# Expert halves by seven products in a third expert, sums kept in PSUM, and float64 weights narrowed through DRAM

## The chip, the cores and the metric

The kernel runs on one core of one Trainium2 chip. The metric is device time in microseconds (us) of one execution, as the median of several runs. Engines are named as in the profile: PE is TensorE (matmul), PEld its weight load, DVE is VectorE, ACT is ScalarE, POOL is GpSimd, SP is the engine whose queue issues all DMAs here.

## The reference, cut to what matters

Blocked causal attention over 4 x 8 heads of 576 rows, then a mixture of four experts in which every token goes through every expert, then a second layer with a softmax-gated activation and a layer norm.

```
x = attention(q, k, v)                        # 2304 tokens x 512
p = domain_probs / sum(domain_probs)
for e in range(4):
    out += p[:, e] * (relu(x @ w1[e]) @ w2[e])    # w1[e]: 512 x 1024, w2[e]: 1024 x 512
h = out @ w_in                                # w_in: 512 x 1024, float64
solu = h * softmax(h)
ln = (solu - mean) / sqrt(var + 1e-6) * g_ln
result = ln @ w_out                           # w_out: 1024 x 512, float64
```

## The kernel before, in words

Tokens are 18 tiles of 128. Every product is done in three float16 products (high x high, high x low, low x high), since each float32 operand x is kept as hi = f16(x) and lo = f16(x - hi). Attention makes the token tiles one after the other; the experts work on tiles that are ready. The tiles are two parts (`PARTS`): 6 tiles in two groups of 3, then 12 tiles in four groups of 3. A phase j is one expert on one part: phases 0 to 3 are experts 0 to 3 on the first part, phases 4 to 7 are experts 0 to 3 on the second part (`e = j % E`). Phases 0 to 3, and part of 4, run beside the attention; from about 450 us on only the experts are left, and from 928 us the second layer (`m2_h`, `m2_o`).

In a plain phase (`phase_units`, 0 to 4 and 7) a group of 384 tokens needs 8 x 12 matmuls of 384 columns for the first product (`emit_h`, L311) and three times 24 matmuls of 512 columns for the second (`emit_o`, L331). ACT takes the relu out of PSUM (L319), DVE the low part (L320), and DVE adds each finished output tile into `acc` (L355).

Phases 5 and 6 (experts 1 and 2) do the first product by halves (`st_units`, L529): both operands are cut in two along rows and columns, and seven products of half the size in each direction stand in for eight, so a group needs 2 chains x 7 products x 12 matmuls of 192 columns. The combined operands are made ahead: `T` from the tokens, once per group (`t_steps`), and `S` from the expert's split weights, once per expert and chain (`s_steps`). Each product has a PSUM tile of its own; DVE adds them up in SBUF (tiles `stu`, seven adds per chain, L541), ACT takes the relu of each result (L547) and DVE its low part (L548), 128 columns x 192 at a time.

Weights are loaded into one staging tile in four parts, squared and scaled on first use, and split by ACT (hi, L263) and DVE (lo, L266) into one of three slots (`w0` to `w2`) that rotate by the counter in `next_w`. All eight phases load both matrices of their expert. `w_in` and `w_out` come as 64-bit words; during phase 7 DVE turns them into float32 in eight pieces of 128x1024 with seven instructions each (L189 to L213).

DMAs are all issued by SP in order, and an issue waits until what it depends on is done, so a waiting issue holds up those behind it. The instruction order of each engine is written out when the program is built: a list scheduler takes instructions by priority and by when their inputs should be ready, and `spread` sets between which units of a phase a background task stands. Relu, low parts and sums have a raised priority (`high_priority`).

Of the kernel before, what the change touches and what calls it, by code (L numbers as in the profile page):

```python
# [7 lines left out]
F32 = mybir.dt.float32  # L8
# [34 lines left out]
GT = 3  # L43

# [14 lines left out]
def tile_kernel(  # L59
# [46 lines left out]
    hp = ctx.enter_context(tc.tile_pool(name="h", bufs=8))  # L106
# [52 lines left out]
    cv = {}  # L159

    def w_steps(key, src, bits, inv, tag, load_eng, rows=None, hi_eng=None, place_raw="stage", known=False):

        n = src.shape[1]
        k = src.shape[0] // 128
        q = k // 4

        wide = src.dtype == I64
        raw = {}

        def load64(c):  # L170
            def f():
                r = cv["pool"].tile([128, 1024, 2], I32, tag="raw64", name="raw64")
                dv = src.bitcast(I32).rearrange("(k p) f -> p k f", p=128)
                load_eng.dma_start(
                    out=r.rearrange("p (k f) w -> p k (f w)", k=q), in_=dv[:, c * q:(c + 1) * q]
                )
                raw[c] = r
            return f

        def to32(c):  # L180

            a = [None, None]

            def words():
                r = raw[c]
                a[0] = cv["pool"].tile([128, 1024], I32, tag="cvA", name="cvA")
                a[1] = cv["pool"].tile([128, 1024], I32, tag="cvP", name="cvP")
                h = r[:, :, 1]
                vec.tensor_scalar(  # L189
                    out=a[0], in0=h, scalar1=3, scalar2=0x3FFFFFF8,  # L190
                    op0=ALU.logical_shift_left, op1=ALU.bitwise_and,
                )
                vec.scalar_tensor_tensor(
                    out=a[0], in0=h, scalar=-0x40000000, in1=a[0], op0=ALU.bitwise_and, op1=ALU.bitwise_or
                )
                vec.tensor_scalar(
                    out=a[1], in0=h, scalar1=0x7FFFFFFF, scalar2=None, op0=ALU.bitwise_and
                )

            def value():  # L200
                top, tmp = a[0].bitcast(F32), a[1].bitcast(F32)
                vec.scalar_tensor_tensor(
                    out=top, in0=a[1], scalar=float(896 << 20), in1=top, op0=ALU.is_ge, op1=ALU.mult
                )
                vec.tensor_scalar(
                    out=a[1], in0=a[0], scalar1=-0x800000, scalar2=None, op0=ALU.bitwise_and
                )
                o = stage[key][:, c * 1024:(c + 1) * 1024]
                vec.scalar_tensor_tensor(
                    out=o, in0=raw.pop(c)[:, :, 0].bitcast(U32), scalar=2.0 ** -52, in1=tmp,  # L210
                    op0=ALU.mult, op1=ALU.mult,
                )
                vec.tensor_tensor(out=o, in0=o, in1=top, op=ALU.add)  # L213

            return [words, value]
# [9 lines left out]
        def load_part(c):  # L225
            def f():
                sv = stage[key].rearrange("p (k f) -> p k f", k=k)
                dv = src.rearrange("(k p) f -> p k f", p=128)
                load_eng.dma_start(out=sv[:, c * q:(c + 1) * q], in_=dv[:, c * q:(c + 1) * q])
            return f  # L230
# [22 lines left out]
        def split(c):  # L253
            def f():
                r = stage[key][:, c * 1024:(c + 1) * 1024]
                hi = wt[key][:, 0].rearrange("p k f -> p (k f)")[:, c * 1024:(c + 1) * 1024]
                lo = wt[key][:, 1].rearrange("p k f -> p (k f)")[:, c * 1024:(c + 1) * 1024]
# [18 lines left out]
        if wide:  # L276
            steps = [load64(0), load64(1), load]
            for c in range(4):
                steps += to32(c)
                if c < 2:  # L280
                    steps.append(load64(c + 2))
# [6 lines left out]

    xT, x2T, acc = {}, {}, {}
    hch = {}  # L290

# [7 lines left out]
    def emit_h(e, t0, k, fs, pool):  # L299
# [5 lines left out]
        h = hp.tile([128, 2, 128 * GT], F16, tag="h", name="hch")  # L305
# [34 lines left out]
    def out_unit(e, t, o0, pool):  # L340
        c = coef_of(e, t)
        ps = emit_o(e, o0, pool)
        k = t - PARTS[part(t)][0]
        with tc.high_priority(offset=PRI):
            if e == 0:
# [10 lines left out]
        if e == E - 1:  # L356
            finish_x2(t)

# [9 lines left out]
    def coef_of(e, t):  # L368
# [4 lines left out]
        if e == 0:  # L373
            c = sp.tile([128, 1], F32, tag="c0", name="c0")
            vec.tensor_scalar(
                out=c, in0=pt[:, t, 0:1], scalar1=c1, scalar2=c2, op0=ALU.mult, op1=ALU.mult
# [25 lines left out]
    def phase_units(j, runs, pool):  # L402

        e = j % E
        units = []
        for t0, k in runs:
# [5 lines left out]
            for t in range(t0, t0 + k):  # L412
                units.append((
                    t, lambda t=t, o=(t - t0) * 128: out_unit(e, t, o, pool), 24 * 0.216,
# [12 lines left out]
    def combine(shape, out, x, y, op):  # L427
# [7 lines left out]
        def high():  # L435
            r["f"] = view(st_["tmp"].tile([128, 512], F32, tag="f", name="stf", bufs=3))
            vec.tensor_tensor(out=r["f"], in0=x(0), in1=y(0), op=op)  # L437

        def low():
# [3 lines left out]
            if "l" not in r:  # L443
                r["l"] = view(st_["tmp"].tile([128, 512], F32, tag="l", name="stl", bufs=1))
# [8 lines left out]
    def t_steps(g):  # L453
# [8 lines left out]

        def place():
            Ts[g] = st_["keep"].tile([128, 4, 2, 2, HT], F16, tag=f"T{g}", name="T")

        sh = (2, HT)
        r1, a1 = combine(sh, T(0), B(0, 1), B(0, 0), ALU.subtract)
        r2, a2 = combine(sh, T(1), B(1, 1), lambda b: None if b else r1["f"], ALU.subtract)
        r3, a3 = combine(sh, T(2), B(1, 1), B(0, 1), ALU.subtract)
        r4, a4 = combine(sh, T(3), B(1, 0), lambda b: None if b else r2["f"], ALU.subtract)  # L470
        return [place] + a1 + a2 + a4 + a3

    def s_steps(e, half):

        def A(i, j):
            return lambda b: wt["w1", e][:, b, 2 * j:2 * j + 2, 512 * i + 256 * half:512 * i + 256 * half + 256]

        def S(k):
            return lambda b: Ss[e, half][:, k, b]
# [4 lines left out]
        sh = (2, 256)  # L484
        r1, a1 = combine(sh, S(0), A(1, 0), A(1, 1), ALU.add)
        neg = lambda b: None if b else r1["f"]
        r2 = {}

        def second():
            r2["f"] = st_["tmp"].tile([128, 512], F32, tag="f", name="stf", bufs=3).rearrange("p (a b) -> p a b", a=2)  # L490
            vec.tensor_tensor(out=r2["f"], in0=r1["f"], in1=A(0, 0)(0), op=ALU.subtract)

        def second_low():
            vec.tensor_tensor(out=r2["f"], in0=r2["f"], in1=A(0, 0)(1), op=ALU.subtract)

        def second_split():
            two_parts(r2["f"], S(1)(0), S(1)(1))

        r3, a3 = combine(sh, S(2), A(0, 0), A(1, 0), ALU.subtract)
        r4, a4 = combine(sh, S(3), A(0, 1), lambda b: None if b else r2["f"], ALU.subtract)  # L500
        return [place] + a1 + [second, second_low, second_split] + a4 + a3

    def st_units(e, g, half, pool):

        key = (1, g)
        t = GROUPS[1][g][0] + GT - 1
        fa = [2 * half, 2 * half + 1]
        fb = [4 + f for f in fa]
        ps, u = {}, {}
# [13 lines left out]
        def product(c, lhs, rhs):  # L523
            ps[c] = pool.tile([128, 512], F32, tag="h", name="hps")
# [10 lines left out]
        W = 2 * HT  # L535

        def add(k, x, y):
            n = {"s": 3, "u": 2}.get(k[0], 1)
            u[k] = st_["tmp"].tile([128, W], F32, tag=k[0] + str(n), name="stu", bufs=n)
            with tc.high_priority(offset=PRI):  # L540
                vec.tensor_tensor(out=u[k], in0=x, in1=y, op=ALU.add)  # L541

        def hidden(x, fs, j):
            with tc.high_priority(offset=PRI):
                for jj, f in enumerate(fs):
                    h, v = hch[f][:, :, HT * j:HT * j + HT], x[:, jj * HT:jj * HT + HT]
                    act.activation(out=h[:, 0], in_=v, func=AF.Relu)  # L547
                    vec.scalar_tensor_tensor(  # L548
                        out=h[:, 1], in0=v, scalar=0.0, in1=h[:, 0], op0=ALU.max, op1=ALU.subtract
                    )  # L550

        def f1():
            for f in fa + fb:
                hch.pop(f, None)
# [877 lines left out]
```

## Time and profile before

| | |
|---|---|
| median of 3 runs | 1122.9 us (1121.86 to 1125.56) |
| profiled execution | span 1118.5 us from its first to its last instruction; the page gives no time of its own for what lies around the span |
| PE busy | 1054.0 us, 94% of the span |
| DVE / ACT / POOL busy | 821.9 / 500.8 / 184.7 us |
| bytes moved by DMA | 125.87 MB, mean 113 GB/s |
| attention with phases 0 to 3 | 0 to about 447 us |
| phases 4, 5, 6, 7 | about 447 to 567, 567 to 684.5, 684.5 to 802.5, 802.5 to 928 us |
| second layer | 928 to 1118.5 us |

PE is busy almost throughout after 250 us; the first quarter of the span has gaps. A matmul's recorded duration overlaps that of the next, so counts and starts tell more about PE's speed than mean durations do. The stage borders are read from the chain of waits, in which L529 (halves) takes over from L311 (plain) and back.

### The profile page before, as it was taken

How to read it: one execution, taken by the hardware profiler on the slowest of the kernel's cores; microseconds unless marked ns; L12 is line 12 of the kernel's file. 1: busy time of each engine (PE TensorE's matmuls, PEld its weight loads, DVE VectorE, ACT ScalarE, POOL GpSimd, SP SyncE). 2: the span in 40 equal slices, each digit the busy share in tenths (PEclk: the TensorE clock that was granted, in tenths of full speed). 3: DMA queues.
4: the chain of work that ended last, by engine and by line, in shares of the span. 5: the costliest groups of instructions: out<-in, count | busy, mean ns of one | idle time of the engine just before them, and what ended most of it. 6: DMA issues, size and time to landing. Idle time of an engine off the chain costs nothing.

```text
span 1118.5 us, 19987 instructions
## 1 busy us (share of the span) xinstructions
PE 1054.0 (94%) x7776; PEld 642.1 (57%) x7776; DVE 821.9 (73%) x1818; ACT 500.8 (45%) x1115; POOL 184.7 (17%) x176
## 2 busy tenths in 40 slices
PE   4479889899998999999999999999999999999998
PEld 4456766466565555655567777766555554444443
DVE  6888787648678678536997459544999656999883
ACT  5657676647655457433542224211324332333222
POOL 4874632323115411000000000000000000000000
PEclk9999999899999999999999999999999999999999
DMA  9868986837648748332150002200422101443343
GB/s 306 236 149 176 248 183 148 246 94 209 174 103 236 152 114 224 74 43 56 33 203 6 1 1 79 73 1 1 148 87 96 38 19 29 89 90 85 76 85 85
DMA packets 216063, 125.87 MB, mean 113 GB/s; under 512 B 183712, under 2 KB 185760, under 8 KB 215456
## 3 DMA queue, kind: packets, MB, share of 16 engines
q1 hardware_dynamic: 215968, 124.59, 43.4%
q8 instruction: 61, 1.00, 0.4%
q14 instruction: 34, 0.28, 0.1%
HBM read 73.18 MB, written 6.29 MB: 71 GB/s over the span
## 4 chain that ended last, share of the span: by engine, by line
PE 73%; DVE 11%; DMA 8%; POOL 4%; issue 3%; ACT 1%; SPq 0%; DVEq 0%; ACTq 0%; POOLq 0%
PE ops L331 27%; PE hps L311 15%; PE hps L529 9%; PE h L1283 8%; PE o L1346 8%; DMA pT<-hl 6%; PE pv L872 3%; DVE wt L266 2%; DVE hl L843 1%; PE sps L799 1%; PE sps L800 1%; DVE stf L437 1%; DMA vraw<-in_vC_dram 1%; POOL wt L259 1%; DVE hch L320 1%
## 5 line engine op out<-in xcount | busy, mean ns | idle before, releaser
L331 PE MATMUL ops<-wt,hch 128*128 128x512 f16 x1728 | 387.6, 379 | 3.9 <-DVE wt L266 1.6
L331 PEld LDWEIGHTS <-hch 128*128 128x128 f16 x1728 | 166.2, 98 | 190.4 <-issue 4.4
L311 PE MATMUL hps<-xT,wt 128*128 128x384 f16 (+1 forms) x1920 | 268.5, 297 | 1.7 <-DVE hch L320 1.3
L311 PEld LDWEIGHTS <-wt 128*128 128x128 f16 x1920 | 164.0, 100 | 85.9 <-issue 4.0
L838 ACT ACTIVATE p<-sps,nm 128x320 f32<-128x320 f32 (+4 forms) x144 | 79.1, 553 | 89.9 <-DVE nm L809 59.6
L843 DVE TENSOR_TENSOR hl<-p,hl 128x320 f16<-128x320 f32 (+4 forms) x132 | 90.5, 699 | 33.2 <-ACT hl L842 32.9
L266 DVE SCALAR_TENSOR_TENSOR wt<-stage,ws,wt 128x1024 f16<-128x1024 f32 x72 | 99.7, 1392 | 8.3 <-ACT wt L263 6.9
L355 DVE SCALAR_TENSOR_TENSOR acc<-ops,coef,acc 128x512 f32<-128x512 f32 x54 | 40.4, 748 | 82.1 <-PE ops L331 82.1
L1283 PE MATMUL h<-wt,x2T 128*128 128x512 f16 x432 | 95.5, 379 | 0.8 <-DVE acc L355 0.8
L319 ACT ACTIVATE hch<-hps 128x384 f16<-128x384 f32 x130 | 62.3, 482 | 75.1 <-PE hps L311 74.6
L1346 PE MATMUL o<-wt,lt 128*128 128x512 f16 x432 | 95.5, 379 | 0.0
L320 DVE SCALAR_TENSOR_TENSOR hch<-hps,hch 128x384 f16<-128x384 f32 x130 | 70.5, 544 | 32.2 <-ACT hch L319 32.2
L799 PE MATMUL sps<-ks,qhi 128*128 128x288 f32 (+3 forms) x160 | 67.4, 424 | 23.7 <-ACT p L838 10.1
L263 ACT ACTIVATE wt<-stage,ws 128x1024 f16<-128x1024 f32 x64 | 71.1, 1140 | 6.0 <-PE hps L311 2.2
L1283 PEld LDWEIGHTS <-x2T 128*128 128x128 f16 x432 | 42.2, 98 | 52.0 <-issue 1.1
L541 DVE TENSOR_TENSOR stu<-stu,hps 128x384 f32<-128x384 f32 x112 | 59.4, 550 | 17.3 <-PE hps L529 17.3
L1346 PEld LDWEIGHTS <-lt 128*128 128x128 f16 x432 | 42.3, 98 | 50.9
L547 ACT ACTIVATE hch<-stu 128x192 f16<-128x192 f32 x128 | 39.2, 354 | 70.4 <-DVE stu L541 70.2
L842 ACT ACTIVATE hl<-p 128x320 f16<-128x320 f32 (+4 forms) x132 | 66.0, 522 | 7.3 <-DMA pT<-hl 6.7
L872 PE MATMUL pv<-v,pT 128*128 128x64 f16 x1392 | 54.8, 197 | 13.6 <-DMA pT<-hl 13.6
L529 PEld LDWEIGHTS <-S 128*128 128x128 f16 x768 | 64.3, 98 | 2.6
L872 PEld LDWEIGHTS <-pT 128*128 128x128 f16 x1392 | 49.4, 101 | 22.6 <-DMA pT<-hl 17.5
(155 smaller groups left out, 1366.7 us busy)
## 6 DMA issues: line engine op xcount, KB each, us to landing
stage<-in_w_dram SPq DMA_DIRECT2D x64, 512.0 KB, 5.9
raw<-in_qT_dram SPq DMA_DIRECT2D x34, 256.0 KB, 3.5
vraw<-in_vC_dram SPq DMA_DIRECT2D x30, 256.0 KB, 3.3
raw<-in_kT_dram SPq DMA_DIRECT2D x24, 288.0 KB, 3.5
raw<-in_w_in_dram SPq DMA_DIRECT2D x4, 1024.0 KB, 4.8
raw<-in_w_out_dram SPq DMA_DIRECT2D x4, 1024.0 KB, 5.0
out_dram<-o2s SPq DMA_DIRECT2D x16, 256.0 KB, 2.5
raw<-in_kT_dram SPq DMA_DIRECT2D x8, 192.0 KB, 4.1
```

Of the source, the lines that this page charges most:

```text
L263: h = bg_(act.activation(out=hi, in_=r, func=AF.Copy, scale=stage[key, "s"]), "A")
L266: stage["last"] = vec.scalar_tensor_tensor(out=lo, in0=r, scalar=stage[key, "s"], in1=hi, op0=ALU.mult, op1=ALU.subtract)
L311: pe.matmul(ps[:, j * n:j * n + n], w[:, a, kk, f * 128:(f + 1) * 128], x[:, b * KD + kk, c0:c0 + n], start=(m == 0), stop=(m == 3 * KD - 1),)
L320: nc.vector.scalar_tensor_tensor(out=h[:, 1, :n], in0=ps[:, :n], scalar=0.0, in1=h[:, 0, :n], op0=ALU.max, op1=ALU.subtract)
L331: pe.matmul(ps, hch[f][:, a, o0:o0 + 128], w[:, b, f, :], start=(m == 0), stop=(m == 3 * KF - 1))
L529: pe.matmul(ps[c][:, jj * HT:jj * HT + HT], lhs(a, kk, jj), rhs(b, kk), start=(m == 0), stop=(m == 5),)
L799: pe.matmul(o, hi[:, h % 4], rhs, start=True, stop=False)
L838: act.activation(out=dst, in_=src, func=AF.Exp, bias=nm[:, j + x:j + x + 1], scale=SCALE, accum_out=sums[:, h:h + 1],)
L843: anc["D"] = vec.tensor_tensor(out=hl[:, W + c0:W + c0 + n_], in0=pf[:, 0:n_], in1=hl[:, c0:c0 + n_], op=ALU.subtract)
L872: pe.matmul(o, tt[:, a * nch + c, :], v[:, bb, hs], start=(m == 0), stop=(m == total - 1))
L1283: pe.matmul(ps[:, half], x[:, a * KD + kk, c:c + 128], w[:, b, kk, half * 512:half * 512 + 512], start=(m == 0), stop=(m == 3 * KD - 1),)
L1346: pe.matmul(ps, tt[:, a * KF + f], w[:, b, f], start=(m == 0), stop=(m == 3 * KF - 1))
```

## The change

- The experts' order is now 0, 1, 2, 3 on the first part and 3, 0, 1, 2 on the second (`ORDER`). Expert 3's weights stay where they are between the two, so seven weight pairs are loaded (`LOADS`), not eight. Expert 3 is the plain phase 4; experts 0, 1 and 2 (phases 5, 6, 7) all go by halves.
- The halves are done in another order with fewer tiles (`st_chain`): a PSUM tile X takes products 1, 6, 5 and 3 one on top of the other, Z takes 7 and 4, Y takes 2. After products 1, 6 and 5 ACT copies X to SBUF; DVE adds three times per chain; the relu and the low part cover 2 x 192 columns in one instruction. Two chains are interleaved, and the next group's first product stands before the last four.
- `S` is made from float32 weights that are loaded again in pieces of 128x2x256 (24 DMAs), by four DVE adds and four splits per chain; the lower-right halves of `w1` that are never used are not loaded or split (`less`).
- `w_in` and `w_out` are narrowed in 16 pieces of 128x512 during the halves' phases (`narrow`) and stored to DRAM; phase 7 loads the float32 back. The pieces' buffers are those of the first part's tokens, so the second-layer inputs of the first part are written to DRAM (`kept`) and fetched back in phase 7.
- `h` has four buffers of double size in place of eight.

```diff
+ORDER = [0, 1, 2, 3, 3, 0, 1, 2]
+LOADS = [j for j in range(len(ORDER)) if j != E]
-    hp = ctx.enter_context(tc.tile_pool(name="h", bufs=8))
+    hp = ctx.enter_context(tc.tile_pool(name="h", bufs=4))
...
+        def product(x, lhs, rhs):
+            first = x not in ps
+            if first:
+                ps[x] = pool.tile([128, 512], F32, tag="h", name="hps")
+            opened = None
             for jj in range(2):
                 m = 0
                 for kk in range(2):
                     for a, b in ((0, 0), (0, 1), (1, 0)):
-                        pe.matmul(
-                            ps[c][:, jj * HT:jj * HT + HT], lhs(a, kk, jj), rhs(b, kk),
-                            start=(m == 0), stop=(m == 5),
+                        start = first and opened is None
+                        i = pe.matmul(
+                            ps[x][:, jj * HT:jj * HT + HT], lhs(a, kk, jj), rhs(b, kk),
+                            start=start, stop=(m == 5), skip_group_check=not first or jj > 0,
                         )
...
+        def f1():
+            product("X", A(0, 0), B(0, 0))
+            copy("b")
+        def f2():
...
+            product("Y", A(0, 1), B(1, 0))
+            result("b", "Y", fa, 0)
+        def f6():
+            product("X", S(1), T(1))
+            copy("u")
+        def f7():
+            product("Z", S(2), T(2))
+        def f5():
+            product("X", S(0), T(0))
+            copy("w")
+            result("w", "Z", fb, 1)
+        def f3():
+            product("X", S(3), B(1, 1))
+            with tc.high_priority(offset=PRI):
+                hidden(ps["X"][:, :W], fa, 1)
+        def f4():
+            product("Z", A(1, 1), T(3))
+            result("u", "Z", fb, 0)
...
+            u = ([a1] if g == 0 else []) + [b1, a2, a6, b2, b6, a7, a5, b7, b5]
+            if g + 1 < len(gs):
+                u.append(chains[g + 1][0][0])
+            u += [a3, b3, a4, b4]
...
+            if g[0] == 0 and o == 128 * (GT - 1):
+                kept[g] = dp.tile([128, 2 * KD, 128 * GT], F16, tag=f"x2{g[1]}", name="kept")
+                sync.dma_start(out=kept[g], in_=x2T[g])
...
+        tasks = [load(0), load(1)]
+        for c in range(8):
+            tasks += [words(c), value(c), store(c)]
+            if c < 6:
+                tasks.append(load(c + 2))
...
+        if j == E - 1:
+            moe += spread(us, (0, 0.1 * n, post))
+            post = []
+            continue
...
-    for j in (5, 6):
+    for j in (5, 6, 7):
...
-    us = phase_units(7, GROUPS[1], psb)
```

Three places show how the instructions move. On PE, in a halves group of 384 tokens in the middle of a phase (`hps` are PSUM tiles, `xT` and `T` tokens, `wt` and `S` weights), the first matmul of each product of one chain stood before as

```order
L529 MATMUL hps_8300<-xT_4890,wt_6684 128x192
...
L529 MATMUL hps_8315<-T_7964,S_7203 128x192
...
L529 MATMUL hps_8330<-xT_4890,wt_6684 128x192
...
L529 MATMUL hps_8350<-T_7964,S_7203 128x192
...
L529 MATMUL hps_8367<-T_7964,S_7203 128x192
...
L529 MATMUL hps_8391<-T_7964,wt_6684 128x192
...
L529 MATMUL hps_8412<-xT_4890,S_7203 128x192
```

and the two chains of a group now stand, after the first chain's first product (`hps_9383`), as

```order
L585 MATMUL hps_9553<-xT_4865,wt_8073 128x192
...
L585 MATMUL hps_9570<-xT_4865,wt_8073 128x192
...
L585 MATMUL hps_9383<-T_7871,S_8719 128x192
...
L585 MATMUL hps_9604<-xT_4865,wt_8073 128x192
...
L585 MATMUL hps_9553<-T_7871,S_8837 128x192
...
L585 MATMUL hps_9637<-T_7871,S_8719 128x192
...
L585 MATMUL hps_9383<-T_7871,S_8719 128x192
...
L585 MATMUL hps_9672<-T_7871,S_8837 128x192
...
L585 MATMUL hps_9553<-T_7871,S_8837 128x192
...
L585 MATMUL hps_9707<-xT_6070,wt_8073 128x192
...
L585 MATMUL hps_9383<-xT_4865,S_8719 128x192
```

Between two products on one tile (`hps_9383`, `hps_9553`) there are three products of 12 matmuls that use others.

On DVE, in the first phase by halves, between the sums (`acc`) of one group and the next, there was only work of the chains (`stu` adds, `hch` low parts):

```order
L355 SCALAR_TENSOR_TENSOR acc<-ops,coef,acc 128x512 x3
L541 TENSOR_TENSOR stu<-stu,hps 128x384 x3
L548 SCALAR_TENSOR_TENSOR hch<-stu,hch 128x192 x2
L541 TENSOR_TENSOR stu<-stu,hps 128x384 x3
L548 SCALAR_TENSOR_TENSOR hch<-stu,hch 128x192 x2
L541 TENSOR_TENSOR stu<-stu,hps 128x384
L548 SCALAR_TENSOR_TENSOR hch<-stu,hch 128x192 x4
L541 TENSOR_TENSOR stu<-stu,hps 128x384 x3
```

Now the pieces of `w_in` and `w_out` (`raw` the words, `cv` the result) stand among the chains' adds (`stc`) and sums:

```order
L378 SCALAR_TENSOR_TENSOR acc<-ops,coef,acc 128x512
L264 SCALAR_TENSOR_TENSOR cv<-raw_8921,cv 128x512
L378 SCALAR_TENSOR_TENSOR acc<-ops,coef,acc 128x512
L275 SCALAR_TENSOR_TENSOR cv<-raw_8921,cv 128x512
L611 TENSOR_TENSOR stc<-stu,hps 128x384
L279 TENSOR_SCALAR raw_8921<-cv 128x512
L261 TENSOR_SCALAR cv<-raw_8957 128x512
L280 SCALAR_TENSOR_TENSOR raw_8921<-raw_8921 128x512
L267 TENSOR_SCALAR raw_8957<-raw_8957 128x512
L611 TENSOR_TENSOR stc<-stu,hps 128x384
```

Fourteen of the 16 pieces end between the first and the last sum of this phase; a piece's first instruction waits for its load, and a piece's load is issued when the piece two before it is done.

On SP, near the end of the attention (`pT` are transposes that PE's attention products wait for), the issues stood as

```order
L89 DMA raw<-in_qT_dram 128x512
L89 DMA stage<-in_w_dram 128x2x512 x4
L89 DMA_TRANSPOSE pT<-hl 128x10x128
L89 DMA_TRANSPOSE x2T<-xh 128x8x128
L89 DMA_TRANSPOSE pT<-hl 128x14x128 x2
```

and now stand as

```order
L91 DMA raw<-in_qT_dram 128x512
L91 DMA_TRANSPOSE x2T<-xh 128x8x128
L91 DMA_TRANSPOSE pT<-hl 128x10x128
L91 DMA kept<-x2T 128x3072
L91 DMA raw_7555<-in_w_in_dram 128x1024
L91 DMA_TRANSPOSE pT<-hl 128x14x128
```

A weight load is gone, and the two new issues wait one for the other: `kept` for the `x2T` transpose, the words' load for `kept`, whose buffer it writes. The same pair stands once more some 12 issues earlier.

## Rows read from the trace of the kernel before

**Rows 1.** The page: span, PE's line of part 1, slices of part 2.
```profile
span 1118.5 us, 19987 instructions
...
PE 1054.0 (94%) x7776; PEld 642.1 (57%) x7776; DVE 821.9 (73%) x1818; ACT 500.8 (45%) x1115; POOL 184.7 (17%) x176
...
PE   4479889899998999999999999999999999999998
...
PEclk9999999899999999999999999999999999999999
```
**Rows 2.** Stages: stretch, length, busy PE, PEld, DVE, ACT, POOL, clock, DMA, GB/s.
```profile
250.00:447.00 197.00, 191.19 (x1492) 113.93 (x1491) 149.34 (x301) 122.24 (x290) 58.07 (x52) 1.00 0.69 174
447.00:567.00 120.00, 120.00 (x855) 69.04 (x854) 78.65 (x162) 51.15 (x97) 1.88 (x2) 1.00 0.26 61
567.00:684.50 117.50, 115.73 (x956) 82.85 (x954) 81.97 (x177) 36.39 (x91) 0.00 (x0) 1.00 0.12 43
684.50:802.50 118.00, 118.00 (x938) 81.96 (x936) 74.34 (x155) 31.98 (x81) 0.00 (x0) 1.00 0.13 48
802.50:928.00 125.50, 124.85 (x677) 66.04 (x675) 94.17 (x166) 47.42 (x89) 0.00 (x0) 1.00 0.25 74
928.00:1118.50 190.50, 186.64 (x864) 84.45 (x863) 153.05 (x470) 54.90 (x75) 0.00 (x0) 1.00 0.36 77
```
**Rows 3.** PE's waits from 447 us on: releaser, us in total, times, longest.
```profile
PE hps L529 <- DVE stu L541: 1.6, 1, 1.6
PE h L1283 <- DVE acc L355: 0.8, 1, 0.8
```
**Rows 4.** The chain that ended last: start, us, what, count.
```profile
714.32 13.86 PE hps L529 x168
728.18 15.54 PE ops L331 x72
...
864.94 15.60 PE hps L311 x96
```
**Rows 5.** DVE back to back, timeline: start, us, instruction.
```profile
540.96 0.68 DVE L437 TENSOR_TENSOR stf<-wt,stf 128x512 f32<-128x512 f16 x1
541.56 0.69 DVE L437 TENSOR_TENSOR stf<-wt 128x512 f32<-128x512 f16 x1
542.16 0.55 DVE L320 SCALAR_TENSOR_TENSOR hch<-hps,hch 128x384 f16<-128x384 f32 x1
542.63 0.68 DVE L425 TENSOR_TENSOR S<-stf,S 128x512 f16<-128x512 f32 x1
...
803.97 0.74 DVE L355 SCALAR_TENSOR_TENSOR acc<-ops,coef,acc 128x512 f32<-128x512 f32 x1
804.63 1.22 DVE L213 TENSOR_TENSOR stage<-stage,cvA 128x1024 f32<-128x1024 f32 x1
...
812.24 0.68 DVE L189 TENSOR_SCALAR cvA<-raw 128x1024 int32<-128x1024 int32 x1
812.84 0.68 DVE L196 TENSOR_SCALAR cvP<-raw 128x1024 int32<-128x1024 int32 x1
```
**Rows 6.** ACT's copy out of PSUM, lines by form: count, busy us, mean ns, idle before.
```profile
L559 ACT ACTIVATE stu<-hps 128x384 f32<-128x384 f32 x16 | 7.7, 479 | 73.7 <-PE hps L529 73.7
```
**Rows 7.** DVE in one of the full stretches, by stretches of 10 us.
```profile
570.00:580.00 10.00, 8.83 (x95) 7.72 (x93) 10.00 (x17) 6.63 (x14) 0.00 (x0) 1.00 0.29 107
```
**Rows 8.** DMA issues: count, KB each, median us from issue to landing.
```profile
stage<-in_w_dram SPq DMA_DIRECT2D x64, 512.0 KB, 5.9
...
raw<-in_w_in_dram SPq DMA_DIRECT2D x4, 1024.0 KB, 4.8
...
acc<-spill SPq DMA_DIRECT2D x6, 256.0 KB, 2.7
...
x2T<-xh SPq DMA_TRANSPOSE x18, 2.7
```
**Rows 9.** PE's waits from 250 to 447 us, the longest.
```profile
PE pv L872 <- DMA pT<-hl: 3.7, 6, 1.6
```

More of the change, by code (lines that the diff above doesn't have):

```diff
@@ L158, in tile_kernel, with w_steps @@
     wt = {}
[L159 to L164, printed above, removed]
+    def w_steps(key, src, bits, inv, tag, load_eng, rows=None, hi_eng=None, place_raw="stage", known=False, less=False):
+        single = key in ("w_in", "w_out")
+        n = F if key == "w_in" else D if key == "w_out" else src.shape[1]
+        k = 4096 // n
         q = k // 4
[L167 to L215, printed above, removed]
@@ L304, in emit_h @@
         w, x = wt["w1", e], xT[g]
-        h = hp.tile([128, 2, 128 * GT], F16, tag="h", name="hch")
+        h = h_tile()
         for j, f in enumerate(fs):
@@ L338, in tile_kernel, with out_unit @@
     spilled = {}
[L340 to L341 removed]
+    def out_unit(e, t, o0, pool, first=False, last=False):
+        c = coef_of(e, t, first)
         ps = emit_o(e, o0, pool)
@@ L355, in out_unit, with fetch_x2 @@
                 vec.scalar_tensor_tensor(out=acc[t], in0=ps, scalar=c, in1=acc[t], op0=ALU.mult, op1=ALU.add)
-        if e == E - 1:
+        if last:
             finish_x2(t)
+            g, o = group(t)
+            if g[0] == 0 and o == 128 * (GT - 1):
+                kept[g] = dp.tile([128, 2 * KD, 128 * GT], F16, tag=f"x2{g[1]}", name="kept")
+                sync.dma_start(out=kept[g], in_=x2T[g])
+    kept = {}
+    def fetch_x2():
+        for g, d in kept.items():
+            x2T[g] = xps[0].tile([128, 2 * KD, 128 * GT], F16, tag=f"xT{g[1]}", name="x2T")
+            sync.dma_start(out=x2T[g], in_=d)
     def fetch():
@@ L471, in t_steps, with load @@
         return [place] + a1 + a2 + a4 + a3
     def s_steps(e, half):
[L475 to L479, printed above, removed]
+        inv = wcol["w1", e]
+        r = {}
+        def load():
+            r["x"] = x = raw4().rearrange("p a (k f) -> p a k f", k=2)
+            r["s"] = sp.tile([128, 1], F32, tag="ss", name="ss")
+            vec.reciprocal(out=r["s"], in_=inv)
+            src = w1[e].rearrange("(j k p) (i f) -> p i j k f", p=128, k=2, i=2)
+            for i in range(2):
+                for j in range(2):
+                    sync.dma_start(out=x[:, 2 * i + j], in_=src[:, i, j, :, 256 * half:256 * half + 256])
@@ L481, in place, with add, f @@
+        def add(o, a, b, op):
+            def f():
+                vec.tensor_tensor(out=r["x"][:, o], in0=r["x"][:, a], in1=r["x"][:, b], op=op)
+            return f
         def place():
             Ss[e, half] = st_["keep"].tile([128, 4, 2, 2, 256], F16, tag=f"S{half}", name="S")
[L484 to L503, printed above, removed]
+        def split(k, a):
+            def f():
+                x, s = r["x"][:, a], r["s"]
+                hi, lo = Ss[e, half][:, k, 0], Ss[e, half][:, k, 1]
+                act.activation(out=hi, in_=x, func=AF.Copy, scale=s)
+                vec.scalar_tensor_tensor(out=lo, in0=x, scalar=s, in1=hi, op0=ALU.mult, op1=ALU.subtract)
+            return f
@@ L533, in product, with copy @@
+                        if start:
+                            opened = i
+                        elif first and m == 0:
+                            after(i, opened)
                         m += 1
[L535 to L539, printed above, removed]
+        def copy(k):
+            u[k] = st_["tmp"].tile([128, W], F32, tag=k, name="stu")
             with tc.high_priority(offset=PRI):
-                vec.tensor_tensor(out=u[k], in0=x, in1=y, op=ALU.add)
@@ L543, in hidden @@
-        def hidden(x, fs, j):
-            with tc.high_priority(offset=PRI):
[L545 to L550, printed above, removed]
-        def f1():
-            for f in fa + fb:
-                hch.pop(f, None)
-                hch[f] = hp.tile([128, 2, 128 * GT], F16, tag="h", name="hch")
-            product(1, A(0, 0), B(0, 0))
-            u["b"] = st_["tmp"].tile([128, W], F32, tag="b1", name="stu", bufs=1)
-            with tc.high_priority(offset=PRI):
-                act.activation(out=u["b"], in_=ps[1][:, :W], func=AF.Copy)
```

242 lines of the change are left out of this document (158 added, 84 removed).

## The prediction

> **What bounds the kernel now.** I read the page first, then the busy times by stage, PE's waits, the chain that ended last, and only then the other engines. The page says that PE is busy 94% of the 1118.5 us span [rows 1]; its gaps lie in the first quarter. The stages show what matters here: from 447 us on PE is idle for 1.8 us in phase 5 (117.5 less 115.73), for 0.65 us at the end of phase 7, and in between not at all [rows 2]. Only two waits stand behind that: one of 1.6 us for a DVE add of the halves and one of 0.8 us for the last `acc` before the second layer [rows 3]. The granted clock is 1.00 in all these stages, the 2.4 GHz level. So from 447 us on the time is the number of matmuls times their spacing, and a change there is worth what it takes from PE, less what it makes PE wait. The chain gives the spacing: a plain group's first product, 96 matmuls of 384 columns, takes 15.60 us (162.5 ns each); a group's halves, 168 matmuls of 192 columns, 13.86 us (82.5 ns each); its second product 15.54 us [rows 4].
>
> The profiled execution's own time is known by its span alone, 1118.5 us. The median of the runs is 1122.9 us, so I count 4.4 us around the span, which the change does not touch, and make the sum as a difference.
>
> **The change part by part.**
>
> *PE.* Phase 7 (now expert 2) goes from plain to halves in four groups: 4 x (13.86 - 15.60) = -6.96 us. Phase 4 stays plain with expert 3, phases 5 and 6 keep their halves, with the same 7 x 12 matmuls per chain. A product that adds to what is in PSUM is a matmul like the others, and no matmul is added. The order of PE during the attention, as far as I compared it, has the same expert work before the same attention products, with pieces of 2 to 3 us moved by a few rows.
>
> A rule of the Trainium skill speaks against this term. "TensorE: Matmul & The Clock Gate", section "Back-to-back issue gap", gives for a stream of weight loads and matmuls in a real kernel about 81 ns at 128 columns and 131 ns at 512, so that narrow matmuls are dear. On a line between the two, 192 columns would cost 89 ns and 384 columns 114 ns, and the halves 4 x (168 x 89 - 96 x 114) = +16 us, an estimate from that page. The trace does not agree: it has 82.5 and 162.5 ns, and 215.8 ns at 512 columns (15.54 us over 72), at the same clock [rows 2, 4].
>
> *Waits of PE in the halves.* New is that a product waits for ACT to copy the tile it adds to. In the order three other products, 3 x 0.99 us, stand between two on one tile. ACT's copy takes 0.48 us [rows 6], so even with one relu of like size ahead of it PE has about 2 us to spare; ACT was busy 32 of 118 us in phase 6 [rows 2]. I count nothing. The cover goes if ACT is late by 2 us at a time; each of 72 such waits would then cost what is above that.
>
> *DVE.* Back to back, DVE's pitch is 0.47 us for 128x384, 0.60 for two sources of 128x512, 0.66 for an `acc` sum, and 0.60 for one source of 128x1024 [rows 5], so about 0.34 for half of that. A halves group now needs 6 adds, 8 low parts and 3 sums: 14 x 0.47 + 3 x 0.66 = 8.6 us, of 29.4 us of PE (13.86 + 15.54). That is light in phases 6 and 7. In phase 5 the narrowing comes on top: a piece is 3 x 0.34 + 4 x 0.60 = 3.4 us, and the order puts 14 pieces between the first and the last sum of that phase. There, DVE has 14 x 3.4 = 48 us of pieces, three groups of chains at 6.6, 12 sums at 0.66, 16 instructions for the next `S` at 0.60 and 4 weight splits at about 1.2: 90 us. PE needs 3 groups x 29.4 plus about 10 us from the first to the last sum of one group, 98 us. So DVE is 92% full with 8 us to spare. What a full DVE costs is seen in the trace: it was full in the end of phase 4 and the start of 5 (10.00 of 10 us [rows 7]), and the single 1.6 us wait is from there [rows 3]. That stretch now has less to do (`S` without the joining of high and low parts), while a full stretch of 98 us follows it. Bounds: -1.6 us if the old wait goes and none comes; +9 us if DVE is late throughout (next part). I take +1.0, nearest to the row of 1.6.
>
> *The pieces' loads.* A piece's first instruction waits for 512 KB that are asked for when the piece two before is done; behind it on DVE stand the chains' adds, and for those waits PE. Loads of 256 KB land after 2.7 us and of 1024 KB after 4.8 [rows 8], so I take 3.5, plus 0.4 for the issue, about 4 us. Adding up the pitches between, the order leaves 2 to 9 us; four places are short, by 1 to 2 us each. That is 4 to 6 us of the 8 to spare: hidden, with little over.
>
> *The next expert's `S`.* One float32 buffer serves both chains, so the second chain's four loads wait until the first chain's are split, which waits for the last product that uses the old `S`. From there to the first product that needs the new second half, PE has the three outputs (15.5 us) and about seven products (7 us). The way is four splits, a load of 4 to 6 us, four adds and four splits at 0.60, with weight splits between: some 20 us by pitch. It fits twice with about 2 us left; a DVE that is late by more passes that on.
>
> *Weights.* One of eight pairs goes: 8 splits on ACT and on DVE and 4 MB of loads, issued near the end of the attention. PE was idle 5.8 us between 250 and 447 us [rows 2], 3.7 us of it for `pT` transposes [rows 9]. At most 5.8 us can be won there. Against it, SP twice waits in its order for an `x2T` transpose (2.7 us), then for the 768 KB `kept` store (between 2.7 and 4.8 us [rows 8]), before `pT` issues behind it. At worst that is 2 x 7.5 us late, though before the attention stage ends there was work for PE at hand. I take 0 for the two together, with -5.8 and +8 as ends. The fetch of `kept` and the reload of the float32 weights fall into phase 7, where DMA was 25% busy [rows 2]; the second layer is unchanged and PE-bound.
>
> **Sum.** -6.96 + 1.0 + 0 = -6.0: 1122.9 - 6.0 = 1116.9, say 1117 us.
>
> **The rivals.**
>
> *The attention gains as well.* If all of the 5.8 us goes, 1122.9 - 7.0 + 1.0 - 5.8 = 1111 us. For it: the load and the eight splits fall in that stage. Against: most of the time that PE waits there is for `pT`, in 6 waits of at most 1.6 us [rows 9], which no split of a weight sets.
>
> *DVE or SP takes part of it back.* DVE has 8 us to spare in phase 5; when its pieces wait 1 us each (14 us), PE loses 6 us there, and the two `S` hand-overs lose 1 to 2 us each: 1122.9 - 7.0 + 8 = 1124, no change. The two `kept` waits, if all of one arrives at PE, give about the same. For it: the order packs DVE to 92%. Against: in phase 7 DVE was busy for 94 of 125.5 us with the same conversion and its loads [rows 2], and PE waited for nothing there but the 0.8 us at its end [rows 3].
>
> *Slower: the pieces' loads are as slow as the weights' loads.* Those take 5.9 us for the same 512 KB [rows 8]. Then a piece waits 5.9 - 3.5 = 2.4 us longer, 14 pieces 34 us, 8 of it hidden: 1122.9 - 7.0 + 26 = 1142 us. It decides from 1.3 us a piece on (18 us less 8, against the 7 won plus 3.4). Against: most of these loads stand in the attention, where DMA was at 0.69 of its time, and phase 5 has 0.12 [rows 2].
>
> *Narrow matmuls are dear.* If the weight loads set the pace of the halves, at 81.96 us over 936 or 88 ns each [rows 2], a group takes 168 x 88 = 14.7 us, phase 7 wins 4 x 0.9 = 3.5 us, and the time is 1122.9 - 3.5 + 1 = 1120.4. Against: 13.86 us for 168 stands in the chain itself [rows 4]. By the Trainium skill's rule above ("Back-to-back issue gap") it would be 1122.9 + 16 = 1139 us.
>
> *The change doesn't do what it says:* if PE waited for every ACT copy in full (72 x 0.7 us), the halves would gain nothing: 1122.9 - 7 + 50. The three products between speak against it; I give it no chance of its own.
>
> **How the numbers follow.** Two runs of this kernel differ by 0.3%, so less than 3.4 us is no change. Forecast 1117 (1113.5 to 1119.4): 0.62. The attention gains as well, near 1111: 0.08. Part taken back, 1119.5 to 1126: 0.22. Slow loads: 0.07. Dear narrow matmuls: 0.01, inside no change. So faster 0.70, the same 0.23, slower 0.07. The range that leaves out 2 in 10 cuts the slower cases, half of those near no change, and the end of the gain: 1112 to 1123 us.
>
> **What would show it.** Right: phase 7 is about 118 us long in place of 125.5; L585 has 2016 matmuls at 82.5 ns of spacing; PE waits in all four phases stay below 4 us; ACT's copies end more than 1 us before the product that follows; DVE is near full in phase 5 and half empty in 6 and 7. Wrong: PE waits for `stc` or `hch` of DVE in phase 5, for `S` at the start of phases 6 and 7, or for `stu` of ACT anywhere; DVE waits for the words' loads by more than 1 us each; `pT` lands later after the two `kept` stores, and the attention ends later.

## The result, and the profile after

The changed kernel takes 1137.3 us (median; 1133.6 to 1138.5) where the kernel before takes 1122.4. The ratio is 1.0128 with a 95% interval of 1.0102 to 1.0155: slower by 15 us, where 1117 us was forecast. The profiled execution took 1138.5 us and has a span of 1136.7 us, 18.2 us more than before [rows 1]; by its span the execution profiled before lies some 2 us under its kernel's median and this one 1 us over it, which makes up the difference to 15 us.

The page after, with the lines that answer to [rows 1]:

```profile
span 1136.7 us, 20546 instructions
...
PE 1058.1 (93%) x8064; PEld 663.6 (58%) x8064; DVE 791.7 (70%) x1758; ACT 513.5 (45%) x1107; POOL 183.3 (16%) x176
...
PE   4588889899999999999899999999999999999998
...
PEclk9999989899999999999999999999999999999999
```

The page hardly shows it: DVE is less busy than before, and PE's slices are as full. The stages show it. The borders are now the end of each phase's last second product (583.3, 711.3, 827.1, 946 us); columns as in [rows 2]:

```profile
250.00:447.00 197.00, 188.26 (x1462) 111.58 (x1461) 135.12 (x287) 107.62 (x267) 55.94 (x52) 0.99 0.68 161
447.00:583.30 136.30, 129.14 (x882) 72.59 (x880) 75.01 (x157) 56.01 (x110) 1.89 (x2) 0.99 0.33 72
583.30:711.30 128.00, 120.30 (x968) 84.27 (x967) 116.41 (x222) 41.34 (x80) 0.00 (x0) 1.00 0.50 159
711.30:827.10 115.80, 115.80 (x938) 81.68 (x937) 58.18 (x95) 41.28 (x76) 0.00 (x0) 1.00 0.18 61
827.10:946.00 118.90, 117.90 (x960) 83.58 (x959) 65.89 (x144) 55.57 (x109) 0.00 (x0) 1.00 0.17 41
946.00:1136.70 190.70, 186.64 (x864) 84.45 (x863) 152.95 (x470) 54.90 (x75) 0.00 (x0) 1.00 0.37 78
```

Phase 7 takes 118.9 us in place of 125.5, the second layer 190.7 as before, and phase 6 has no wait at all. So the gain arrived in full. But phase 4's last second product ends at 583.5 us, where that of the kernel before ends at 568.1, and phase 5 has 7.7 us in which PE is idle (128.00 less 120.30). PE's waits from 400 us to the second layer (who waited for whom: us in total, times, longest), to be held against the two waits of [rows 3] and the 3.7 us of [rows 9]:

```profile
PE pv L940 <- DMA pT<-hl: 6.0, 4, 2.6
PE hps L585 <- DVE stc L611: 5.9, 7, 1.8
PE hps L334 <- DVE hch L343: 3.3, 3, 2.5
PE hps L585 <- ACT stu L598: 1.5, 4, 0.8
```

Each of the first three lines is a place of its own: `pT` in the attention, low parts late in phase 4, adds of the chains in phase 5.

**First, `pT` late beside the words' loads.** SP's queue near 400 us (start, us, issue), and PE there:

```profile
393.74 1.24 SPq L91 DMA_TRANSPOSE x2T<-xh  x1
397.19 0.34 SPq L91 DMA_DIRECT2D kept<-x2T  x1
397.57 2.50 SPq L91 DMA_TRANSPOSE xT<-xh  x1
402.11 0.33 SPq L91 DMA_DIRECT2D raw<-in_w_in_dram  x1
402.55 1.22 SPq L91 DMA_TRANSPOSE pT<-hl  x1
```

```profile
407.08 0.52 PE L940 MATMUL pv<-v,pT 128*128 128x64 f16 x12 [2.60 <-DMA pT<-hl]
407.44 3.79 PE L334 MATMUL hps<-xT,wt 128*128 128x384 f16 x12
```

`kept` starts only when the `x2T` transpose has landed, the words' load only when `kept` has landed, and `pT` stands behind both. But the order on SP is the smaller part of the delay here. DVE finishes `pT`'s input `hl` at 402.12 us and `pT` is issued at 402.55, 0.4 us later. What is long is its way to landing, 4.5 us right behind the load of 512 KB (KB each, us from issue to landing):

```profile
raw<-in_w_in_dram SPq DMA_DIRECT2D x1, 512.0 KB, 4.0
pT<-hl SPq DMA_TRANSPOSE x1, 4.5
```

There is a second way from the load to `pT`. The instruction that DVE runs first of each of the first two pieces (L267) stands in the attention and waits there for its words, with the softmax behind it (`hl`, and the row maximum `nm`, from which the next `pT` are made):

```profile
406.20 0.43 DVE L267 TENSOR_SCALAR raw<-raw 128x512 int32<-128x512 int32 x1 [2.60 <-DMA raw<-in_w_in_dram]
...
407.01 0.35 DVE L911 TENSOR_TENSOR hl<-p,hl 128x192 f16<-128x192 f32 x1
...
447.22 0.43 DVE L267 TENSOR_SCALAR raw<-raw 128x512 int32<-128x512 int32 x1 [4.63 <-DMA raw<-in_w_in_dram]
...
447.63 1.08 DVE L873 TENSOR_REDUCE nm<-sps 128x2 f32<-128x896 f32 x1
```

PE waits 2.6 us for the first of these transposes. Behind the second load, issued at 443.05 us, it waits three times, at last 2.29 us at 462 us; there `pT` is issued 2.1 us after its input is ready (443.50 and 441.42 us), so that SP's order counts for more. Right behind the waits of 2.6 and 2.29 us the granted clock is 0.50, the 1.2 GHz level (these two stretches by the same columns as the stages), so that 12 matmuls of 384 columns take 3.79 us in place of 1.95 (12 x 162.5 ns):

```profile
407.60:411.00 3.40, 3.40 (x13) 1.67 (x11) 1.50 (x4) 1.49 (x5) 0.00 (x0) 0.50 0.29 58
...
462.20:465.60 3.40, 3.40 (x30) 2.03 (x31) 0.96 (x2) 0.23 (x1) 0.00 (x0) 0.50 0.38 75
```

Half of 3.4 us lost twice makes 3.4 us more, as much as one more wait.

**Second, DVE before a load, late in phase 4.** DVE's order there, and the product of PE that waited:

```profile
553.37 1.00 DVE L343 SCALAR_TENSOR_TENSOR hch<-hps,hch 128x384 f16<-128x384 f32 x2
560.26 1.42 DVE L536 TENSOR_TENSOR raw<-raw 128x512 f32<-128x512 f32 x2 [5.89 <-DMA raw<-in_w_dram]
561.60 0.55 DVE L343 SCALAR_TENSOR_TENSOR hch<-hps,hch 128x384 f16<-128x384 f32 x1
```

```profile
562.20 2.11 PE L334 MATMUL hps<-xT,wt 128*128 128x384 f16 x12 [2.50 <-DVE hch L343]
```

DVE stands 5.89 us before the first add of the second half's `S`, whose float32 weights have not landed, and a low part of the plain phase stands behind it. That low part frees the buffer for PE's next product. The first product that uses this phase's `S` starts at 584.4 us.

**Third, a full DVE in phase 5.** DVE is busy for 116.41 of 128 us there, and in its fullest stretch for 36.61 of 38:

```profile
592.00:630.00 38.00, 36.51 (x314) 26.98 (x314) 36.61 (x72) 12.67 (x27) 0.00 (x0) 1.00 0.54 167
```

The seven waits for `stc` are all in phase 5; phases 6 and 7 have the same chains and 58 and 66 us of DVE work, and no such wait. PE's spacing is what it was: in phase 6 the chain of waits has

```profile
739.60 13.86 PE hps L585 x168
753.46 15.54 PE ops L354 x72
```

as in [rows 4].

### The profile page after: what moved, and what is told of

It reads as the page before. It is cut to its first block, busy times and chain, and to the rows that moved or that the text cites. A ratio compares the mean times of both kernels' runs of the same rounds, so it can differ in the third digit from the quotient of the medians.

```text
span 1136.7 us, 20546 instructions
## 1 busy us (share of the span) xinstructions
PE 1058.1 (93%) x8064; PEld 663.6 (58%) x8064; DVE 791.7 (70%) x1758; ACT 513.5 (45%) x1107; POOL 183.3 (16%) x176
## 4 chain that ended last, share of the span: by engine, by line
PE 62%; DMA 17%; DVE 12%; POOL 4%; issue 3%; ACT 1%; SPq 1%; DVEq 0%; ACTq 0%; POOLq 0%
PE ops L354 22%; PE hps L585 9%; PE hps L334 9%; PE h L1358 8%; PE o L1421 8%; DMA pT<-hl 8%; PE pv L940 3%; DMA raw<-in_w_in_dram 2%; DMA raw<-in_w_out_dram 2%; DVE wt L223 2%; PE sps L867 1%; DMA stage<-in_w_dram 1%; PE sps L868 1%; DMA raw<-in_w_dram 1%; SPq L91 1%
## 5 line engine op out<-in xcount | busy, mean ns | idle before, releaser
L334 PE MATMUL hps<-xT,wt 128*128 128x384 f16 (+1 forms) x1536 | 208.4, 292 | 5.9 <-DVE hch L343 5.1
L334 PEld LDWEIGHTS <-wt 128*128 128x128 f16 x1536 | 128.2, 101 | 66.3 <-issue 9.8
L585 PEld LDWEIGHTS <-S 128*128 128x128 f16 x1152 | 96.1, 98 | 8.3 <-issue 5.8
L223 DVE SCALAR_TENSOR_TENSOR wt<-stage,ws,wt 128x1024 f16<-128x1024 f32 (+1 forms) x64 | 85.5, 1349 | 8.3 <-ACT wt L220 6.9
L585 PE MATMUL hps<-T,S 128*128 128x192 f16 x864 | 76.5, 246 | 4.4 <-DVE stc L611 3.3
L585 PEld LDWEIGHTS <-wt 128*128 128x128 f16 x864 | 72.8, 98 | 9.3 <-issue 3.5
L598 ACT ACTIVATE stu<-hps 128x384 f32<-128x384 f32 x72 | 34.1, 482 | 89.8 <-PE hps L585 89.8
L343 DVE SCALAR_TENSOR_TENSOR hch<-hps,hch 128x384 f16<-128x384 f32 (+1 forms) x98 | 52.7, 540 | 26.6 <-ACT hch L342 26.5
L603 ACT ACTIVATE hch<-stc 128x384 f16<-128x384 f32 x72 | 37.1, 521 | 71.2 <-DVE stc L611 71.1
```

Source lines behind the costliest of these rows:

```text
L223: stage["last"] = vec.scalar_tensor_tensor(out=lo, in0=r, scalar=stage[key, "s"], in1=hi, op0=ALU.mult, op1=ALU.subtract)
L334: pe.matmul(ps[:, j * n:j * n + n], w[:, a, kk, f * 128:(f + 1) * 128], x[:, b * KD + kk, c0:c0 + n], start=(m == 0), stop=(m == 3 * KD - 1),)
L343: nc.vector.scalar_tensor_tensor(out=h[:, 1, :n], in0=ps[:, :n], scalar=0.0, in1=h[:, 0, :n], op0=ALU.max, op1=ALU.subtract)
L585: i = pe.matmul(ps[x][:, jj * HT:jj * HT + HT], lhs(a, kk, jj), rhs(b, kk), start=start, stop=(m == 5), skip_group_check=not first or jj > 0,)
```

## The experiments

The theory was that these three places have three causes, each in the order of an engine or a queue and none in the new arithmetic. Its rivals: the attention is late for other reasons; the waits of phases 4 and 5 come from one backlog of DVE; three products between two on one tile are too few. Each gain below is the difference of two medians, 1137.3 us less the kernel's; by the intervals of the ratios a gain is known to some 4 us. So a gain that differs from the expected one by a microsecond or two says nothing, and whether a wait is gone is read from the trace.

**Kept's stores behind the attention.** The edit takes the stores out of the attention and makes them follow its last transpose; the words' loads follow by themselves, since they write the same buffers:

```diff
-                sync.dma_start(out=kept[g], in_=x2T[g])
+                to_keep.append(g)
...
+    for g in to_keep:
+        after(sync.dma_start(out=kept[g], in_=x2T[g]), marks["pT"])
```

> The changed kernel with the two stores of kept issued behind the last pT transpose of the attention instead of among them (the words' first two loads, which write the same buffers, follow behind them). Theory, the order on SP's queue: in the changed kernel PE waited 2.6 us at 407 us and 2.3 us at 462 us for pT transposes that stood behind kept and the words' load, and right behind each the granted clock was 0.5 for 3.4 us, 1.7 us lost each time. So 2.6 + 2.3 + 1.7 + 1.7 = 8 us less: 1137.3 - 8 = 1129 us, with the clock at 1.00 from 210 us on. Rival, the attention is late for other reasons (fewer h buffers, one weight load gone, other splits on DVE), and the transposes only show it: 1136 to 1138 us.

Measured: 1131.0 us (1129.5 to 1136.2), 6.3 us less, ratio to before 1.0083 (1.0061 to 1.0105). PE's waits from 380 to 540 us, and the same stretch of the clock:

```profile
PE pv L941 <- DMA pT<-hl: 0.8, 2, 0.5
PE ops L354 <- DVE hch L343: 0.3, 1, 0.3
```

```profile
400.00:420.00 20.00, 19.20 (x138) 10.35 (x136) 11.96 (x33) 10.24 (x31) 1.89 (x2) 1.00 0.49 102
```

Both waits and both slow stretches are gone. The clock does not stay at 1.00, as was expected: behind a wait of 2.31 us for a low part at 553 us it is 0.50 for 3.4 us. New is also a wait of 2.67 us at 542 us for a sum of ACT (below), and the waits for `stc` in phase 5 are 8.4 us in this trace. 6.3 and the 8 expected lie within the noise of each other.

**Only the words' loads behind the attention.** To tell the words' loads from the stores, `kept` stays in its place:

```diff
-                sync.dma_start(out=r[:, 0:1024], in_=sv[:, c * 512 // n, x:x + 1024])
+                after(sync.dma_start(out=r[:, 0:1024], in_=sv[:, c * 512 // n, x:x + 1024]), marks["pT"])
```

> The changed kernel with only the words' first two loads issued behind the attention's last pT transpose; kept's two stores stay where they were, each waiting for its x2T transpose. With both moved 6.3 us were won. Theory, it is the chain of the two waits on SP (the store for the transpose, 2.2 us, then the load for the store, 4.5 us) that makes pT late, and the second is the longer: 4 to 6 us less than 1137.3, 1131 to 1133 us. Rival, kept's own wait for x2T is enough to make pT late: 1135 to 1137 us.

Measured: 1132.4 us (1130.8 to 1135.2), 4.9 us less, ratio 1.0089 (1.0067 to 1.0111). From 380 to 530 us one line of waits is left, and the `pT` issued at 401.69 us, with no load ahead of it, lands after 2.7 us:

```profile
PE pv L941 <- DMA pT<-hl: 0.8, 2, 0.5
...
pT<-hl SPq DMA_TRANSPOSE x1, 2.7
```

So it was the words' loads that made `pT` late; `kept` alone, waiting for its transpose, costs PE nothing that these rows show. The theory behind the expectation, the load's wait on SP, is not shown by this: the edit takes away at once that wait, the transfer just ahead of `pT`, and DVE's standing at the words (DVE has no wait for them from 400 to 470 us in this kernel). By the rows above SP's wait made 0.4 us of it at the first place. No run parts the three.

**S of the first expert by halves behind the low parts.** The adds of `S` are put later in the program and made to follow the low part that stands before them; the steps that make `T` of the first group, once spread over the whole stretch with `S`, are drawn to its start:

```diff
-    for _, u, _ in spread(moe, (0, len(moe), t_steps(0) + s_steps(ORDER[5], 0) + s_steps(ORDER[5], 1))):
+    for _, u, _ in spread(moe, (0, 0.2 * n, t_steps(0) + s0[:1]), (0.4 * n, 0.6 * n, s0[1:] + s1[:1]), (0.8 * n, n, s1[1:])):
...
+                if o == 3 and "low" in marks:
+                    after(x, marks["low"])
```

> The changed kernel with the adds and splits that make S of the first expert by halves put behind the low parts of phase 4 that stand before them in the program: on DVE seven low parts then stand between the first half's S and the second half's, where three stood. Loads and work are the same. Theory, DVE's order: in the changed kernel DVE stood 5.9 us at 554 us waiting for the second half's float32 weights, with a low part behind it for which PE waited 2.5 + 0.6 us and more in the same place, 3.8 us in all; the backlog (T of the next groups, weight splits) then cost some of the waits at 590 to 602 us, 1.8 us. So 4 to 6 us less: 1131 to 1133 us. Rival, the waits come from DVE's amount of work, and only move to the first chains at 584 us, whose S is now later: 1136 to 1139 us.

Measured: 1130.2 us (1129.2 to 1135.4), 7.2 less, ratio 1.0071 (1.0050 to 1.0091). DVE at the same place:

```profile
562.52 0.56 DVE L343 SCALAR_TENSOR_TENSOR hch<-hps,hch 128x384 f16<-128x384 f32 x1 [1.56 <-ACT hch L342]
562.99 2.14 DVE L536 TENSOR_TENSOR raw<-raw 128x512 f32<-128x512 f32 x3
```

The loads are there before DVE comes, the low parts are on time, and PE's waits for `hch` fall from 3.3 to 0.2 us. The waits for `stc` are smaller too, though nothing was changed in phase 5 (565 to 946 us):

```profile
PE hps L587 <- DVE stc L613: 3.6, 3, 2.4
```

The changed kernel has 5.9 us of them and the two kernels with `kept` or the words moved have 8.4 and 6.7, so part of phase 5's waits was probably the backlog of this place.

**The narrowing spread over phases 5 and 6.** Each piece's first instruction follows the last add of a chain before it in the program:

```diff
+                if "add" in marks:
+                    after(x, marks["add"])
...
-                vec.tensor_tensor(out=c, in0=u[k], in1=ps[x][:, :W], op=ALU.add)
+                marks["add"] = vec.tensor_tensor(out=c, in0=u[k], in1=ps[x][:, :W], op=ALU.add)
```

> The changed kernel with each of the 16 pieces of the narrowing put on DVE behind the last add of the chains that stands before it in the program, so that 8 pieces fall into phase 5 and 8 into phase 6, where 14 to 16 ended in phase 5. Loads and work are the same. Theory, a full DVE in phase 5: PE waited there 5.9 us for adds of the chains and 1.5 us for copies behind them, none of it in phases 6 and 7. With 27 us of pieces less in 118 us this goes: 5 to 7 us less, 1130 to 1132 us. Rival 1, the waits come from DVE standing at the pieces' loads (8.6 us in the changed kernel), which stay: half of the waits move to phase 6, 1135 us. Rival 2, they are the cost of the new order of the products (three products between two on one tile are too few): no change, 1137 us.

Measured: 1129.2 us (1125.0 to 1132.8), 8.2 less, ratio 1.0044 (1.0022 to 1.0066). PE's waits in the halves, from 565 to 930 us, are

```profile
PE hps L587 <- DVE stc L613: 2.5, 2, 1.9
PE hps L587 <- ACT stu L600: 0.5, 1, 0.5
```

and DVE is busy 88 of 117 us in the first phase and 85 of 120 in the second. Both lines lie in phase 5, where they add up to 3.0 us against 7.1 in the changed kernel; none moved to phase 6. So most of the waits were not the order of the products, which is the same. Nor were they DVE's standing at the pieces' loads: that grew from 8.5 us to 33.7 (560 to 830 us), and PE waited less.

```profile
DVE raw L269 <- DMA raw<-in_w_in_dram: 18.2, 6, 5.8
DVE raw L269 <- DMA raw<-in_w_out_dram: 15.5, 7, 4.3
```

The edit does two things, it halves the pieces in phase 5 and puts each piece behind the adds of its chains; no run parts them. PE's waits account for some 4 of the 8.2 us; the rest is within the noise of the medians.

**All three.**

> The three edits together: kept's stores behind the attention, S of the first expert by halves behind the low parts, the narrowing spread over phases 5 and 6. Theory, three places each with its own wait: the gains add, 8 + 5 + 6 = 19 us less than the changed kernel, 1118 us, 4 us faster than the kernel before. Rival, the three share a backlog of DVE, so that the second and the third edit win the same waits: 1123 to 1126 us.

Measured: 1118.4 us (1116.4 to 1122.9), ratio to before 0.9965 (0.9943 to 0.9986). The three alone won 6.3 + 7.2 + 8.2 = 21.7 us, together 19.0. Within the noise they add up, and the rival's 1123 to 1126 us is missed. One place is left. From 480 to 910 us PE waits for:

```profile
PE hps L336 <- ACT acc L375: 2.7, 1, 2.7
PE hps L589 <- ACT stu L602: 0.4, 1, 0.4
```

The first line, in the timeline: a load of 1.92 us of issues, DVE 7.19 us before it, ACT behind DVE, and a sum of PE's finished tile behind ACT's split:

```profile
530.92 1.92 SPq L91 DMA_DIRECT2D raw<-in_w_dram  x4
...
538.56 2.15 DVE L538 TENSOR_TENSOR raw<-raw 128x512 f32<-128x512 f32 x3 [7.19 <-DMA raw<-in_w_dram]
...
539.29 2.17 ACT L550 ACTIVATE S<-raw,ss 128x512 f16<-128x512 f32 x3 [8.22 <-DVE raw L538]
...
541.37 0.67 ACT L375 ACTIVATE acc<-ops,c 128x512 f32<-128x512 f32 x1
```

**The first half's S later too.** The same remedy once more, on ACT as well as on DVE:

```diff
-(0.4 * n, 0.6 * n, s0[1:] + s1[:1]), (0.8 * n, n, s1[1:])
+(0.55 * n, 0.7 * n, s0[1:] + s1[:1]), (0.85 * n, n, s1[1:])
...
-                act.activation(out=hi, in_=x, func=AF.Copy, scale=s)
+                after(act.activation(out=hi, in_=x, func=AF.Copy, scale=s), marks["acc"])
```

> The kernel with all three edits, and the first half's S of the first expert by halves put some matmul blocks later too, behind the sums of the first group on ACT and its next low parts on DVE. In the kernel with the three edits PE waited 2.7 us at 542 us for ACT's sum, which stood behind a split of S that waited for the float32 weights' load, and the granted clock was 0.5 for 3.4 us right behind it, 1.7 us lost. Theory, the same kind of wait once more: 4.4 us less than that kernel's 1118.4, 1114 us, with no wait of PE over 0.5 us from 410 us to the second layer. Rival, the later S is late for the first chains: 1118 to 1121 us, with a wait of the halves' products at 570 us.

Measured: 1115.1 us (1114.4 to 1117.2), ratio to before 0.9935 (0.9919 to 0.9951): 7.4 us faster than the kernel before, and the fastest of all. Against the kernel with the three edits it is 3.3 us less, a gain that is barely clear of noise (intervals 0.9919 to 0.9951 and 0.9943 to 0.9986). The waits that are left from 410 us to the second layer:

```profile
PE hps L589 <- ACT stu L602: 1.0, 1, 1.0
PE hps L589 <- DVE stc L615: 0.4, 1, 0.4
```

One of them is 1.0 us long, twice what was expected; the 2.7 us are gone.

**Phase 7 plain again.** On the kernel with the three edits, to weigh the halves alone:

```diff
-    for j in (5, 6, 7):
+    for j in (5, 6):
...
+    us = phase_units(7, GROUPS[1], psb)
```

> The kernel with the three edits, but phase 7 (expert 2 on the second part) plain again as in the kernel before; everything else stays. Theory, PE's count: 4 groups x (15.60 - 13.86) us = 7.0 us more than 1118.4, 1125.4 us. Rival, the products by halves gain less than their count since they wait for copies and adds elsewhere: 1119 to 1122 us.

Measured: 1124.2 us (1122.6 to 1129.1), ratio to before 1.0016 (1.0001 to 1.0030) against 0.9965 with the halves: 0.51% or 5.7 us, known to some 3 us. Phase 7 in this kernel, and with the halves (in the kernel with the three edits):

```profile
806.00:931.00 125.00, 124.37 (x673) 65.75 (x672) 55.41 (x119) 46.16 (x87) 0.00 (x0) 1.00 0.20 51
```

```profile
806.00:924.70 118.70, 117.69 (x958) 83.49 (x957) 66.60 (x145) 57.61 (x113) 0.00 (x0) 1.00 0.19 48
```

6.3 us between them, against 7.0 by count.

## Why the prediction was wrong

The forecast was wrong in sign. Its main term was right. Three waits, taken at 0, 0 and 1.0 us, cost 6.3, 7.2 and 8.2 us by what was won when each was taken away.

- *PE, -6.96 us.* Right: 5.7 us by time, 6.3 us by the stage, and the spacing of the chain is the old one. The rival of dear narrow matmuls falls with it; a group's 168 matmuls take 13.86 us as before. The Trainium skill's figures for a stream of weight loads and matmuls ("TensorE: Matmul & The Clock Gate", section "Back-to-back issue gap") do not hold in this kernel, where 192 columns take 82.5 ns and 512 columns 215.8.
- *The copies of ACT, 0.* Nearly right: 1.5 us in four waits, 1.2 of it in phase 5 and 0.3 in phase 7, and 0.4 us once in the kernel with the three edits. Three products between two on one tile is not true of every pair: by the list in the diff `b5` and `b3` have two between them, and one in a phase's last group. No run changes that order.
- *Weights and `kept`, taken as 0 with 8 us as the upper end.* This step failed. SP's two waits were found, priced at 2.7 and up to 4.8 us, and then dismissed with "before the attention stage ends there was work for PE at hand". That work stood behind the late `pv` in PE's order (the matmuls at 407.44 us), and PE waited with it. The way was also another than the one priced. SP's waits made the first `pT` only 0.4 us late and the second 2.1; the words' load ahead of it went with a landing after 4.5 us in place of 2.7, and DVE stood 2.60 and 4.63 us at the words with the softmax behind it. That a piece's first instruction can hold up what stands behind it was counted for phase 5 and not for the attention. Won by taking it away: 6.3 us. The clock's share, 3.4 us, was in no term.
- *The next expert's `S`, "it fits twice with about 2 us left".* This step looked in the wrong place. It priced the hand-overs from phase 5 to 6 and 6 to 7, which indeed cost little. The first making of `S`, in phase 4, was counted as less work for DVE than before, but not as a wait for a load with other instructions behind it. Taking that away won 7.2 us, and 3.3 us more with the first half's `S` later. The first of the four loads was issued at 553.27 us and DVE went on at 560.26, 7 us, where 4 to 6 were taken.
- *DVE in phase 5, +1.0 us with 9 as the upper end.* The mechanism and DVE's share were right: 116 of 128 us busy, 91%, where 92% was reckoned, and the waits are for DVE's adds. The size failed: 8.2 us won by spreading the pieces, some 4 of them seen as waits of PE. The value was taken from the row that was nearest, a single 1.6 us wait in a stretch of 10 us; but a phase of 128 us at 91% had seven waits for adds, of up to 1.8 us. It also had no room for a backlog from phase 4.
- *The pieces' loads as slow as the weights' loads.* No: the medians to landing were 3.7 and 4.5 us in phase 5. DVE's waits for them came to 8.5 us there, and the kernel with the pieces spread shows that such waits need not cost PE anything.
- *The attention gains as well.* No: with the stores and loads moved PE waits 3.9 us for `pT` from 250 to 447 us, as before.

One reading of the prediction was off without harm: the 4.4 us "around the span" are 1.8 us in the runs on record (1138.5 against a span of 1136.7). Its sum was a difference, so nothing hung on it.

The rival that DVE or SP takes part back was the right one in kind. It had 8 us, since it added DVE's part to two small hand-overs, or took one of SP's waits, but not all the places together; the three edits won 19 us and a fourth 3.3 more, 22.3 in all, and what is then left (1115.1) is the forecast of 1117 and a little less. That it comes so near proves little, since the gains are known to a few microseconds only. Of the 25 us that the profiled execution loses against the count of its matmuls (18.2 + 7.0), 16.6 are PE's idle time from 250 us on (the stages above against [rows 2]) and 3.4 the two slow stretches; where the other 5 went is open.

## What to carry to other kernels

When a change moves work to an engine that has time for it, ask of each moved instruction what it waits for and what stands behind it in that engine's order, and give it a place behind the urgent work that is ready earlier. An engine's share over a phase does not answer this: DVE was idle for 5.9 us and late by it. When several small waits are each possible, the sum of their upper ends is a case of its own and should have a chance; here it came true.

## What was not expected of the hardware

The granted clock fell behind short waits of PE in a stage where, in the changed kernel, it had been at 1.00 for nearly 200 us. From 380 us on, the traces of the changed kernel and of five experiments (the stores, the words, S, the pieces, all three) have 14 waits of PE of 2.2 us or more. With 10 of them came a stretch at 0.50, the 1.2 GHz level, of 3.4 us (once 6.8, with the longest wait, 3.35 us); with the other 4, of 2.2 to 2.7 us, the clock stayed at 1.00. Length does not decide it: the wait of 2.67 us at 542 us has the slow stretch in the kernel with all three edits and not in the one with the stores alone, and a shorter one of 2.0 us at the same place has it in the kernel with phase 7 plain. What decides is not shown. So such a wait cost up to 1.7 us more, once 3.4, than the profile's line of waits says.
